# U and V's halves loaded with a cast by GpSimd's queue, two steps moved to GpSimd, and a new written-out order, in an attention and mixer kernel

## The chip, the cores and the metric

The kernel runs on one core of a Trainium2 chip. The metric is the device time of one execution in microseconds (us), as a median of several runs. A profile shows one execution: TensorE (PE, with its weight loads PEld), VectorE (DVE), ScalarE (ACT), GpSimd (POOL) and the DMA queues of SyncE (SP) and of GpSimd.

## The reference

Causal local attention with a few global keys, then a mixer over tokens of low rank, then an MLP. Cut to what matters:

```python
B, H, S, D = 4, 8, 768, 64          # n_global = 8, n_local = 96, rank = 32
keep = is_global | is_local          # a query sees 96 keys back and the first 8
scores = where(keep, scale * q @ k.T - slope[h] * dist, -1e9)
a = softmax(scores)
x = (a @ v)                          # [B, S, 512], heads side by side
h = x.transpose(0, 2, 1) @ U @ V     # U [768, 32], V [32, 768]
u = x + h.transpose(0, 2, 1)
out = u + relu(u @ w_ch1) @ w_ch2    # w_ch1 [512, 2048], w_ch2 [2048, 512]
```

## The kernel before

All work is cut into some 1100 named steps, each with an engine. A list, `ORDER`, names them all in one order; each engine runs its own steps in the order in which they stand in that list. A planner in the kernel walks the list with a cost for each step. It gives each step a start, PSUM banks and buffers, and puts filler matmuls on zeros (L1327, function `idle`) where it expects PE to wait in the early part. The dictionary `CFG` holds a letter for each choice of engine (A ACT, D DVE, P GpSimd, S a DMA by SP, Q a DMA by GpSimd).

The work goes over 4 batches, and in a batch over 4 pairs of heads, p = 0 to 15. The steps of a pair p, with the lines at which they show in the profile:

- `lk`, `lq`, `lv`: loads of k, q and v, cast from float32 to float16 by DMAs of GpSimd's queue (L450 for pairs 1 to 3, L454 as two halves of 96 KB for later pairs, L458 for v). Pair 0 comes in float32 by SP (L468) and is cast by `Ck`, `Cq`. Buffers are few (3 for q, 3 for k), so a load waits for an earlier pair's transpose. At most 8 DMAs of a queue are under way.
- `TK`, `TQ`: transposes on PE (L594, L575 for pairs 1 to 3). `EK`, `EQ`: their eviction from PSUM (L359 on ACT, L361 on DVE, a helper's lines). `KO`, `VC`, `VG`: copies of k and v for the blocks off the diagonal.
- `SB` (L697, pairs 0 to 3, the bias by a matmul), `S` (L716, scores in three groups .0 to .2), `EX` (L781, exp on ACT), `MK` (mask by DVE, from pair 4 on).
- `PV` (L848, L849), `RC` (reciprocal), `NM` (L887, normalisation into `x_sb`), `XC` (cast of x to float16, `x16`). The last pair of batch 0 does this in thirds (`PV3.0`, `RC3.0`, `NH3.0`, ...).
- `UP`: on PE, x is transposed (L822) and multiplied with U. There are two forms. For the pairs in `CFG["NU"]` x is the stationary operand and U moves, 32 columns at a time (L827); then come `XE`, an eviction into `xus`, and `XU`, one transpose (L928). For the others U, repeated four times, is stationary and x moves, 128 columns at a time (L832).
- `TE`: eviction of x'U into `tmp`. `HM` (L946): times V, added onto the transposed x. With letter R in `CFG["HR"]` its two halves use 64 rows each and run side by side on PE, with F they use all rows one after the other. `E0`, `E1`: eviction of the sum into `uT`.

Changing between matmuls on all rows and matmuls on half the rows costs PE a short pause.

Then the batch's MLP. `M1a` to `M1d` are the first product (L1000 for halves, L1024 for the four blocks done at full width), `RL`, `RM` its ReLU on ACT. Half of it in batches 1 and 2 and three quarters in batch 3 goes by a Strassen-like scheme (`ZP`, L1095, with sums `ZU` to `ZX`, `ZA` to `ZR`). The second product is in seven parts `P1` to `P7` (L1226) of three row blocks, with `RS` (L1218) ahead, `PA`, `PB` for sums, and `DA` to `DH` (L1238, L1265, L1278) adding onto `x_sb`. `O` stores a row block (SP). The weights come in quarters, `w1_0` to `w1_3` (L503) and `w2_0` to `w2_3` (L506), through GpSimd's queue between the pairs' loads. `CFG["OS"]` lists stores that are issued in two pieces.

U and V: `mixl` loads both in float32 by SP (L509, L510) into a part of `x_sb`. `u16` (ACT) makes the float16 copy of U, four times. `vz` clears `vs`, and `vs0`, `vs1`, `vs2` fill it: V's halves, and their difference (L521). `back` is a small memset that ties `mixl` to a place in the order.

GpSimd's queue at first, before: `ones2 wz iota lk1 ones0 lq1 lk3 lq2 ones3 lv0 lk2 lq3 ones1 lv1 lk5 lv3 lv2 lq5 lk4 lq4 w1_0 lk7 w1_3 lv4 lq6 w1_2 lq7 w1_1 lk6 lv5`.

PE at first, before: `... TQ3 SB2.1 S2.1 SB2.2 S2.2 PV1 SB3.0 S3.0 SB2.0 S2.0 SB3.1 S3.1 SB3.2 S3.2 TK5 TQ5 PV2 UP0 TK4 UP1 HM0 PV3.0 PV3.1 PV3.2 TQ4 UP2 HM1 HM2 UP3.0 UP3.1 UP3.2 M1a0.3 M1c0.3 HM3 S4.1 M1d0.3 TK7 M1b0.3 ...`

Of the kernel before, what the change touches and what calls it, by code (L numbers as in the profile page):

```python
# [21 lines left out]
lk0 ones2 wz iota lq0 lk1 ones0 vz relf lq1 rel3 lk3 lq2 bias1 ones3 lv0 bias0 SB0.2 SB0.1 Ck0.1 Cq0.0 bias2 bias4  # L22
Ck0.0 TK0 EK0.1 lk2 Cq0.1 TQ0 EQ0.0 SB0.0 lq3 EK0.0 KO0.1 KO0.0 EQ0.1 mask1 S0.0 EX0.0 TK1 S0.1 EX0.1 EK1 S0.2 KO1
TQ1 EQ1 ones1 lv1 back SB1.1 TK3 EK3 KO3 VC0 mask5 VG0 EX0.2 lk5 lv3 lv2 lq5 lk4 SB1.2 S1.1 EX1.1 S1.2 TQ2 EQ2 lq4
SB1.0 w1_0 S1.0 EX1.0 TK2 EK2 KO2 lk7 VC1 w1_3 PV0 RC0 EX1.2 lv4 VG1 TQ3 EQ3 SB2.1 S2.1 EX2.1 lq6 SB2.2 S2.2 EX2.2
PV1 NM0 SB3.0 S3.0 EX3.0 RC1 NM1 SB2.0 S2.0 w1_2 EX2.0 mixl u16 XC0 VC2 VC3 VG3 SB3.1 S3.1 EX3.1 SB3.2 S3.2 EX3.2
VG2 vs0 vs1 TK5 EK5 XC1 TQ5 PV2 RC2 NM2 UP0 TE0 TK4 EK4 UP1 TE1 XC2 EQ5 HM0 E00 PV3.0 PV3.1 PV3.2 RC3.2 RC3.0 NH3.2
TQ4 EQ4 NH3.0 UP2 TE2 HM1 E01 HM2 E02 RC3.1 NH3.1 KO4 NM3 UP3.0 UP3.1 UP3.2 TE3 M1a0.3 M1c0.3 mask0 HM3 E03 KO5 S4.1
E13 EX4.1 lq7 M1d0.3 TK7 M1b0.3 RL0.3 M1b0.14 M1b0.15 M1a0.2 M1c0.2 M1a0.15 EX4.2 M1a0.13 vs2 TD0 M1a0.14 MK4.2 VC4
VG4 w1_1 RM0.15 RM0.14 RL0.15 mask2 S4.0 EX4.0 MK4.1 EK7 M1d0.2 M1b0.2 RL0.2 MK4.0 RL0.14 M1b0.13 mask3 KO7 ZS5  # L30
M1a0.10 M1b0.12 RM0.12 RM0.13 RL0.10 TQ6 PV4 M1a0.11 M1b0.11 RL0.13 EQ6 RC4 NM4 XC4 TQ7 EQ7 ZS7 RL0.11 RM0.11 lk6
lv5 S5.0 S5.1 EX5.0 MK5.0 EX5.2 M1a0.8 M1b0.10 RM0.10 PA0.3 PB0.3 M1a0.9 RL0.9 w2_2 EX5.1 MK5.1 M1b0.5 RM0.5 M1a0.0
M1c0.0 w2_0 M1d0.0 M1b0.0 MK5.2 VC5 VG5 TK6 EK6 RL0.8 M1a0.4 M1b0.4 RL0.0 M1b0.7 RM0.7 w2_1 w2_3 ZS6 M1b0.6 UP4 PV5
RM0.6 XE4 KO6 RL0.4 M1b0.8 RM0.4 XU4 TE4 lv7 M1a0.5 RM0.8 M1a0.6 RC5 NM5 TWa0 TWb0 RL0.6 M1a0.7 M1a0.1 M1c0.1 M1d0.1
M1b0.1 RL0.7 RL0.5 PA0.1 RL0.1 PA0.0 M1b0.9 RM0.9 M1a0.12 S7.0 RL0.12 PB0.1 PA0.2 PB0.2 EX7.0 RS0.0 HM4 E04 P10.0
XC5 P20.0 S6.1 EX6.1 EX6.2 RS0.1 P10.1 P20.1 UP5 XE5 PB0.0 TWa1 DA0.0 TWb1 lq8 TQ8 EQ8 lk8 TK8 EK8 lq10 P30.0 DF0.0
XU5 DA0.1 P30.1 DF0.1 mask4 MK6.1 MK6.2 P50.0 lv6 lq9 VC7 TE5 HM5 mask6 KO8 S6.0 EX6.0 E05 P60.0 DB0.0 lk9 mask7
lk10 lv8 P60.1 DB0.1 lv11 S7.1 RS0.2 EX7.1 MK6.0 MK7.0 EX7.2 MK7.2 P10.2 P70.0 TK9 EK9 TQ9 EQ9 MK7.1 VC6 DA0.2 VG6
TQ10 EQ10 P50.1 TK10 EK10 P70.1 DC0.0 lq11 VG7 PV7 DD0.1 KO9 PV6 RC7 NM7 P20.2 XC7 lk11 RC6 NM6 P60.2 DB0.2 P30.2
UP7 XC6 VC8 VG8 P40.1 UP6 P70.2 XE6 XU6 TE6 ZS4 XE7 XU7 lk12 TE7 DD0.0 P40.0 DC0.1 O0.1 HM6 E06 HM7 E17 DF0.2 DG0.1  # L40
ZP11.5 DD0.2 P40.2 ZU1.5 DG0.0 E07 ZT1 S8.0 EX8.0 S8.1 O0.0 EX8.2 EX8.1 KO10 P50.2 M1a1.3 TK11 DC0.2 EK11 O0.3
ZP11.4 ZU1.4 DG0.2 ZP61.5 ZW1.5 ZP21.5 ZA1.5 O0.2 O0.4 M1b1.3 RL1.3 KO11 TQ11 lq13 ZP61.4 ZW1.4 EQ11 ZP21.4 ZA1.4
ZP51.5 MK8.0 MK8.2 S9.1 EX9.1 ZP71.4 ZX1.4 ZP71.5 ZX1.5 M1a1.7 EX9.2 ZP51.4 ZB1.4 ZB1.5 M1a1.6 ZP41.4 ZR1.4 ZP41.5
ZR1.5 MK8.1 RL1.6 ZP31.4 ZP31.5 ZD1.4 ZP11.6 ZU1.6 ZP21.6 M1b1.7 RL1.7 PV8 ZD1.5 lv10 RM1.7 ZP11.7 ZU1.7 M1b1.6
MK9.2 ZP61.6 ZW1.6 M1a1.2 M1b1.2 RM1.6 ZP61.7 RL1.2 MK9.1 ZP71.6 ZW1.7 M1a1.4 RL1.4 ZA1.6 O0.5 RC8 ZQ1.5 NM8 XC8 UP8
XE8 ZQ1.4 PA1.1 lv9 VC10 VC9 S9.0 EX9.0 lv12 ZP21.7 ZP71.7 ZX1.7 ZV1.4 ZV1.5 PA1.2 PB1.2 XU8 TE8 M1b1.4 RM1.4 M1b1.5
RM1.5 ZP51.6 HM8 E08 ZA1.7 ZX1.6 TK12 TD1 EK12 ZP41.7 ZR1.7 M1a1.5 RL1.5 VG9 ZB1.6 ZP51.7 ZB1.7 M1a1.0 ZV1.6 M1b1.0
RL1.0 ZV1.7 ZP31.6 M1a1.1 M1b1.1 MK9.0 lq12 TQ12 ZP31.7 VC11 ZP41.6 VG11 ZD1.6 ZQ1.6 EQ12 ZD1.7 ZQ1.7 RL1.1 ZR1.6
PA1.3 RS1.1 S10.1 EX10.2 EX10.1 PA1.0 PB1.0 S10.0 EX10.0 PB1.3 KO12 P21.1 P11.1 PV9 P51.1 RC9 NM9 PB1.1 DA1.1 S11.0
EX11.0 RS1.0 P21.0 P51.0 P11.0 DA1.0 XC9 S11.1 EX11.2 EX11.1 MK11.0 P31.0 DF1.0 MK11.2 P61.1 MK10.0 UP9 XE9 lq14  # L50
TQ14 EQ14 MK11.1 P31.1 DF1.1 P61.0 DB1.0 XU9 TE9 PV11 RC11 lk14 TK14 EK14 lk15 HM9 DB1.1 P71.0 E09 P71.1 lv14 VC14
S12.0 EX12.0 RS1.2 NM11 KO14 DD1.1 DC1.0 P11.2 lk13 DD1.0 S12.1 EX12.1 EX12.2 P41.0 P21.2 MK10.1 VG10 MK10.2 PV10
TK13 EK13 DA1.2 XC11 VC12 DG1.0 P31.2 RC10 TQ13 P61.2 NM10 XC10 DF1.2 VG14 UP11 DB1.2 DC1.1 O1.1 EQ13 UP10 lq15
MK12.2 P71.2 XE11 XU11 XE10 DD1.2 XU10 KO13 TE10 P41.1 DG1.1 HM10 TE11 TD2 E010 HM11 E011 E111 ZT2 S14.0 EX14.0
P51.2 ZP12.6 ZU2.6 P41.2 DC1.2 O1.4 DG1.2 O1.3 S14.1 EX14.1 MK14.1 EX14.2 MK14.2 M1a2.1 M1b2.1 RL2.1 ZP62.6 ZW2.6
M1b2.5 RM2.5 TQ15 TK15 M1b2.4 EK15 M1a2.5 KO15 RM2.4 ZP12.7 RL2.5 ZP52.6 EQ15 ZU2.7 O1.5 ZP72.6 ZX2.6 M1a2.4 M1a2.3
M1b2.3 MK12.0 VG12 MK12.1 PV12 ZB2.6 ZP32.6 ZV2.6 MK14.0 RL2.4 RL2.3 RC12 ZD2.6 ZP62.7 ZP22.7 ZW2.7 ZP12.4 ZA2.7
ZP52.7 ZP42.6 ZU2.4 ZP72.7 ZR2.6 ZP62.4 ZP22.6 ZX2.7 M1a2.0 M1b2.0 O1.2 O1.0 NM12 ZB2.7 ZP32.7 ZA2.6 XC12 ZQ2.6 lv15
VC15 VG15 ZW2.4 PV14 ZD2.7 ZP12.5 RC14 ZP72.4 RL2.0 NM14 XC14 UP12 XE12 ZU2.5 ZP22.5 ZA2.5 PA2.0 ZP62.5 ZW2.5 ZX2.4
M1a2.7 ZP22.4 ZA2.4 XU12 TE12 ZP72.5 ZP52.4 ZB2.4 ZV2.4 ZP42.7 RL2.7 ZV2.7 HM12 ZR2.7 ZQ2.7 ZP42.4 M1a2.2 ZX2.5 E012  # L60
M1b2.2 RL2.2 PA2.3 ZP42.5 ZR2.5 ZP52.5 ZB2.5 ZP32.4 ZD2.4 ZQ2.4 ZV2.5 UP14 XE14 M1b2.7 ZR2.4 RM2.7 ZP32.5 XU14 TE14
ZD2.5 ZQ2.5 M1b2.6 RM2.6 PA2.2 PB2.2 M1a2.6 RL2.6 HM14 E014 RS2.1 P12.1 S13.1 EX13.1 PA2.1 RS2.0 P12.0 DA2.0 P22.0
P22.1 EX13.2 P62.0 P52.1 S15.1 EX15.2 PB2.3 PB2.0 PB2.1 DB2.0 DC2.1 P32.0 DA2.1 P72.0 MK13.1 DF2.0 P32.1 DF2.1
EX15.1 P62.1 MK15.1 lv13 S13.0 S15.0 EX15.0 MK13.2 MK15.2 RS2.2 P12.2 MK15.0 P52.2 EX13.0 MK13.0 P32.2 PV15 DD2.0
P22.2 VC13 VG13 PV13 DA2.2 P62.2 DB2.1 P72.1 RC15 NM15 XC15 UP15 RC13 NM13 XC13 UP13 DB2.2 P72.2 DD2.1 XE15 XU15
XE13 XU13 DF2.2 ZS3.3 TE15 P52.0 DD2.2 ZS3.2 HM15 TE13 HM13 TD3 E115 P42.1 DG2.1 P42.2 E013 ZP13.5 ZP13.2 ZU3.2 E015
P42.0 ZT3 ZP13.4 M1a3.0 ZU3.4 ZU3.5 O2.1 ZP63.2 ZW3.2 DG2.0 DC2.2 DC2.0 O2.3 O2.2 DG2.2 O2.5 M1b3.0 ZP63.5 ZP23.2
ZA3.2 RL3.0 ZP63.4 ZP73.2 ZW3.4 ZP13.3 ZU3.3 ZP23.4 ZA3.4 ZP23.5 ZW3.5 ZA3.5 ZP73.4 ZP13.7 ZX3.2 ZX3.4 ZU3.7 ZP63.3
ZW3.3 ZP53.4 ZB3.4 M1a3.1 M1b3.1 RL3.1 ZP63.7 ZP73.5 ZX3.5 ZP33.4 ZD3.4 ZQ3.4 ZP73.3 ZX3.3 ZP53.5 ZB3.5 ZV3.5 ZP53.3
# [35 lines left out]
class Planner:  # L105
# [57 lines left out]
    def run(self, names):  # L163
        if sorted(names) != sorted(self.names):
            raise RuntimeError("order and tasks differ")
        clock = {PE: 0.0, ACT: 2.0, DVE: 0.7, POOL: 0.75, SP: 0.7}
        lanes = {POOL: [0.0] * self.LANES, SP: [0.0] * self.LANES}
        mode = 0
        dma_free = {POOL: 6.1, SP: 0.0}
        shared_port = {POOL: [], DVE: []}  # L170
        for t in (self.names[n] for n in names):
            r = 0.0
            for d in t.deps:
                r = max(r, d.end + (0.0 if t.eng == d.eng and d.size == 0.0 else d.lat))
            r = max([r] + [g.read for g in t.bw] + [g.written for g in t.br])
# [6 lines left out]
            if t.size:  # L182
                r = max(r, lanes[t.eng][t.parts - 1])
# [1195 lines left out]
```

## Time and profile before

| | |
|---|---|
| time, median of 3 runs | 225.0 us (224.84 to 225.39) |
| the profiled execution | 225.68 us, span of the trace 223.9 us |
| PE, DVE, ACT, POOL busy | 217.5, 182.3, 143.5, 68.9 us |
| PE clock granted | 1.00 |
| DMA | 23.97 MB, 107 GB/s on average; 160 to 200 GB/s in the first 67 us |

The span runs from the first to the last instruction of the trace; the execution's time has 1.8 us more around it. A busy PE includes filler and the modelled ends of matmuls. For each group the page gives its count, the busy time, the mean of one, and what ended the idle time before it. The landing time of a DMA is when the last of its 16 parts has arrived.

### The profile page before, as it was taken

To read this page: it belongs to the slowest core of one execution; us is meant where nothing else is said; L and a number is where in the kernel's file an instruction comes from. 1 tells how busy PE (TensorE), PEld (TensorE's weight loads), DVE (VectorE), ACT (ScalarE), POOL (GpSimd) and SP (SyncE) were. 2 spreads that over 40 slices of the span, in tenths; PEclk is the share of its full clock that TensorE was granted. 3 is DMA by queue.
4 is the path that set the end of the run, shared out by engine and by line. 5 is a ranking of instruction groups with operands and counts; after the bars stand their busy time and mean duration, and the time that the engine had idled before them with its cause. 6 is when DMAs were issued, how large, how long until landed. Compare 5 with 4: busy or idle time off the path is not lost.

```text
span 223.9 us, 6008 instructions
## 1 busy us (share of the span) xinstructions
PE 217.5 (97%) x2446; PEld 160.8 (72%) x2446; DVE 182.3 (81%) x407; ACT 143.5 (64%) x251; POOL 68.9 (31%) x90
## 2 busy tenths in 40 slices
PE   8997999999999999999999999999999999999993
PEld 3754876675888976666788886666688976658883
DVE  5876957889998887997987888788888995888892
ACT  6889697887877378787855567668732347882000
POOL 8876976634964400191221400012000000000000
PEclk9999999999999999999999999999999999999999
DMA  6999999999999987399090941609100104000035
GB/s 172 174 176 146 181 182 185 193 206 161 169 149 73 157 151 223 97 115 71 0 107 12 108 123 52 200 12 70 39 3 3 47 3 187 0 4 0 0 116 215
DMA packets 88763, 23.97 MB, mean 107 GB/s; under 512 B 76416, under 2 KB 86528, under 8 KB 88736
## 3 DMA queue, kind: packets, MB, share of 16 engines
q0 software_dynamic: 69888, 13.64, 73.8%
q1 hardware_dynamic: 18848, 9.95, 15.7%
q8 instruction: 19, 0.31, 0.6%
q14 instruction: 8, 0.07, 0.1%
HBM read 27.46 MB, written 6.29 MB: 151 GB/s over the span
## 4 chain that ended last, share of the span: by engine, by line
PE 90%; DMA 4%; POOL 2%; issue 1%; ACT 1%; DVE 0%; DVEq 0%; POOLq 0%
PE ps L1226 34%; PE ps L1095 14%; PE ps L1000 13%; PE ps L1024 8%; PE ps L716 4%; DMA stgq<-in_q_dram 4%; PE ps L594 4%; PE ps L822 3%; PE ps L849 2%; PE ps L848 2%; PE ps L946 2%; PE ps L1327 1%; PE ps L1218 1%; PE ps L697 1%; POOL stgk L454 1%
## 5 line engine op out<-in xcount | busy, mean ns | idle before, releaser
L781 ACT ACTIVATE ep<-ps 128x1024 f16<-128x1024 f32 (+1 forms) x48 | 43.9, 952 | 14.8 <-PE ps L716 14.5
L1226 PEld LDWEIGHTS <-htr 128*128 128x128 f16 x392 | 36.2, 98 | 6.7 <-issue 2.3
L1238 DVE TENSOR_TENSOR x_sb<-x_sb,ps 128x256 f32<-128x256 f32 (+1 forms) x60 | 26.9, 464 | 7.5 <-PE ps L1226 7.1
L1000 PE MATMUL ps<-uT,w 128*128 128x384 f16 x176 | 32.4, 326 | 0.0
L1226 PEld LDWEIGHTS <-sA 128*128 128x128 f16 x288 | 27.3, 98 | 3.5
L458 POOL DMA_DIRECT2D vt<-in_v_dram x16 | 16.6, 1046 | 30.7 <-PE ps L849 27.3
L1000 PEld LDWEIGHTS <-w 128*128 128x128 f16 x176 | 16.7, 98 | 10.5
L1226 PE MATMUL ps<-w,sA 128*128 128x256 f16 x192 | 24.2, 273 | 0.0
L1226 PE MATMUL ps<-tB,htr 128*128 128x256 f16 (+1 forms) x200 | 23.8, 268 | 0.0
L1226 PE MATMUL ps<-w,htr 128*128 128x256 f16 x192 | 23.5, 273 | 0.0
L1006 ACT ACTIVATE htr<-ps 128x384 f16<-128x384 f32 x44 | 20.8, 492 | 4.1 <-PE ps L1000 3.5
L454 POOL DMA_DIRECT2D stgk<-in_k_dram x24 | 19.8, 845 | 9.9 <-PE ps L594 5.0
L454 POOL DMA_DIRECT2D stgq<-in_q_dram x24 | 20.0, 844 | 5.6 <-DMA w<-in_moe_w_ch_dram 3.4
L1024 PE MATMUL ps<-uT,w 128*128 128x384 f16 x112 | 21.3, 326 | 0.0
L1113 DVE TENSOR_TENSOR htr<-ps,zu 128x384 f16<-128x384 f32 x30 | 16.1, 554 | 6.1 <-PE ps L1095 4.6
L794 DVE TENSOR_TENSOR ep<-ep,mask 128x1024 f16<-128x1024 f16 x24 | 15.9, 684 | 2.9 <-ACT ep L781 2.9
L359 ACT ACTIVATE zu<-ps 128x384 f32<-128x384 f32 x30 | 14.4, 492 | 4.2 <-PE ps L1095 4.0
L887 DVE TENSOR_TENSOR x_sb<-ps,rcp 128x768 f32<-128x768 f32 x16 | 15.2, 953 | 0.4
L1024 PEld LDWEIGHTS <-w 128*128 128x128 f16 x112 | 10.6, 98 | 6.8
L1095 PEld LDWEIGHTS <-w 128*128 128x128 f16 x108 | 10.1, 98 | 6.2 <-issue 0.3
L1042 ACT ACTIVATE htr<-ps 128x768 f16<-128x768 f32 x14 | 11.3, 811 | 4.7 <-PE ps L1024 4.5
L716 PE MATMUL ps<-qT,kT 64*128 64x128 f16 x192 | 14.0, 217 | 0.0
(127 smaller groups left out, 442.3 us busy)
## 6 DMA issues: line engine op xcount, KB each, us to landing
out_dram<-x_sb SPq DMA_DIRECT2D x17, 256.0 KB, 2.4
w<-in_moe_w_ch_dram POOLq DMA_DIRECT2D x8, 512.0 KB, 10.6
vt<-in_v_dram POOLq DMA_DIRECT2D x16, 192.0 KB, 6.6
stgk<-in_k_dram POOLq DMA_DIRECT2D x24, 96.0 KB, 5.8
stgq<-in_q_dram POOLq DMA_DIRECT2D x24, 96.0 KB, 6.1
out_dram<-x_sb SPq DMA_DIRECT2D x13, 128.0 KB, 1.9
vo<-vt SPq DMA_DIRECT2D x8, 165.0 KB, 2.5
kO<-kT SPq DMA_DIRECT2D x6, 120.0 KB, 2.7
```

What stands on the lines that cost most here:

```text
L454: nc.gpsimd.dma_start(o[:, i], src[b, h0 + i].rearrange("(n p) d -> p n d", p=P))
L458: nc.gpsimd.dma_start(vt[gv.slot][:, :, :, 0:D], v[b, h0:h0 + 2].rearrange("h (n p) d -> p h n d", p=P),)
L716: nc.tensor.matmul(t[:, hi, j * P:(j + 1) * P], lhs, qt[r, i * P:(i + 1) * P], start=not biased, stop=True, skip_group_check=biased,)
L781: nc.scalar.activation(ep[gep.slot][:, :, lo:512], ps[:, gsc.slot:gsc.slot + 2, lo:512], AF.Exp, scale=qk_scale)
L794: nc.vector.tensor_tensor(ev, ev, mv, ALU.mult)
L1000: nc.tensor.matmul(ps[:, g.slot, 0:HS], w1[:, dc, jt * P:(jt + 1) * P], ub[:, dc, i * HS:(i + 1) * HS], start=(dc == 0), stop=(dc == NDC - 1),
L1006: nc.scalar.activation(htr[:, jt, i * HS:(i + 1) * HS], ps[:, g.slot, 0:HS], AF.Relu)
L1024: nc.tensor.matmul(ps[:, g.slot + half, 0:HS], w1[:, dc, jt * P:(jt + 1) * P], ub[:, dc, half * HS:(half + 1) * HS], start=(dc == flat[0]) ...
L1095: nc.tensor.matmul(bank(g), a()[:, i], bq[:, i], start=first and i == 0, stop=last and i == 1, skip_group_check=True,)
L1113: return lambda: nc.vector.tensor_tensor(o, x(), y(), ALU.add)
L1226: nc.tensor.matmul(o if part is None else o[:, part], a[:, j, c0 + cols.start:c0 + cols.stop], bq[:, j] if part is None else bq[:, j, part ...
L1238: nc.vector.tensor_tensor(o, o, x, ALU.add)
```

## The change

U is loaded by one DMA of GpSimd's queue straight into `u16` with a cast, without the fourfold copy (`CFG["U16"]` A to Q). V's halves come likewise into `vs` (`vs0`, `vs1`: Q); `vs2`, the difference, is built on GpSimd (P) from V, which `mixl` still loads in float32, later. All 16 pairs are in `NU`, so pairs 0 to 3 take the form of `UP` with `XE` and `XU` (eight new steps). `HM` of pairs 2, 9 and 12 goes from F to R. x of pair 2 is cast by GpSimd (`XC`: P). Several evictions change between ACT and DVE, two more stores are split, and `ORDER` is written anew. The planner is told of one more rule on DMA issues and a start of 5.6 instead of 6.1 for GpSimd's queue. `RC` names the `NM` two pairs earlier, on the same engine, as an input.

```diff
-    "NU": (4, 5, 6, 7, 8, 9, 10, 11, 12, 13, 14, 15),
+    "NU": (0, 1, 2, 3, 4, 5, 6, 7, 8, 9, 10, 11, 12, 13, 14, 15),
...
-    "OS": ((0, 0), (0, 1), (0, 2), (0, 3), (0, 4)),
-    "ZR": "DDAADDDA", "TE": "ADAAAAAAAAAAAADA", "XE": "DDDDDAADADAADAAA", "EK": "ADDDDDADADADDAAD", "EQ": "DDAAAADDAAADDAAD", "KO": "ADDDDDADSSSSASDS",
-    "HR": "FRFRRRRRFFRRFRRR", "U16": "A", "VS": "DAD", "C0": "ADDADADA", "EKS": "ADDADADA", "EQS": "DDDADADA", "KOS": "ADDADADA",
-    "VO": "DDDDDDDSSSSSDSSS", "XC": "DDDDDAAADADQADQA", "E": "AAAAAAAAAAAAAAAA",
+    "OS": ((0, 0), (0, 1), (0, 2), (0, 3), (0, 4), (0, 5), (1, 0)),
+    "ZR": "DDDDADDD", "TE": "ADDDAAAAAAAAAADD", "XE": "DAAAAAAAAAADAAAA", "EK": "ADDAAADDAAADAAAD", "EQ": "DDDADDDDAAADDAAA", "KO": "ADDDADSDSSASSSAS",
+    "HR": "FRRRRRRRFRRRRRRR", "U16": "Q", "VS": "QQP", "C0": "DDADDADA", "EKS": "DADADADA", "EQS": "AADADADA", "KOS": "DDDADADA",
+    "VO": "DDDDDDASSSSSSSAA", "XC": "DDPDDADADADQAAQD", "E": "AAAAAAAAAADAAAAA",
...
     def load_mixer():
-        nc.sync.dma_start(uf, moe_U.rearrange("(c p) r -> p c r", p=P))
+        if not uq:
+            nc.sync.dma_start(uf, moe_U.rearrange("(c p) r -> p c r", p=P))
         nc.sync.dma_start(vf, moe_V)
...
+            if e is None:
+                nc.gpsimd.dma_start(o, moe_V[:, g * HS:(g + 1) * HS])
...
+        c_u16 = add(
+            POOL, 0.84, lambda: nc.gpsimd.dma_start(u16[:, :, 0], moe_U.rearrange("(c p) r -> p c r", p=P)), size=0.8, name="u16",
+        )
```

The new order, engine by engine, where the text speaks of it:

- GpSimd: `ones0 wz iota lk1 lq1 lk2 lq2 lv0 lk3 ones2 ones1 lv1 u16 vs0 lq3 lv2 lq5 ones3 lv3 lk5 lk4 vs1 lq4 w1_3 lk7 XC2 lq7 w1_0 lq6 w1_2 lv4 lk6 w1_1 lv5 w2_0 vs2 w2_2 w2_1 w2_3 lk8 ...`
- PE: `SB0.2 TK0 SB0.1 SB0.0 TQ0 TK1 S0.2 S0.0 TQ1 S0.1 TK2 SB1.1 SB1.0 S1.0 S1.1 TQ2 SB1.2 S1.2 PV0 TK3 SB2.0 S2.0 SB2.1 S2.1 SB2.2 S2.2 TQ3 PV1 SB3.1 SB3.0 S3.1 S3.0 PV2 SB3.2 S3.2 UP0 UP1 TK5 PV3.0 PV3.1 XU0 TK4 XU1 TQ5 HM0 PV3.2 HM1 UP2 UP3.0 UP3.1 UP3.2 XU2 XU3 TQ4 HM2 HM3 S4.1 TK7 S4.0 M1a0.15 M1b0.15 M1b0.12 M1b0.14 TQ7 M1b0.13 M1a0.2 ...`, and at the end `... P33.1 P43.0 P43.2b P43.2a P43.1` (before: `... P73.2 P43.0 P43.1 P43.2a P43.2b`)
- ACT after the first exp: `EX0.2 EX0.0 EX0.1 EX1.0 EX1.1 EX1.2 EK3 EX2.0 EX2.1 EQ3 EX2.2 EX3.1 EX3.0 EX3.2 XE1 EK5 TE0 EK4 E00 E01 XE2 XE3 KO4 E02 E13 EX4.2 ...` (before: `EX0.0 EX0.1 mask5 EX0.2 EX1.1 EQ2 EX1.0 EX1.2 EQ3 EX2.1 EX2.2 EX3.0 EX2.0 u16 EX3.1 EX3.2 vs1 TE0 EQ5 E00 EQ4 TE2 E01 E02 TE3 mask0 E13 EX4.1 ...`)
- DVE there: `... NM2 VC3 VG3 XE0 back RC3.0 RC3.1 NH3.1 TE1 EQ5 NH3.0 RC3.2 NH3.2 NM3 TE2 TE3 EQ4 E03 ...`
- SP: the last stores are `O3.5a O3.5b O3.5c O3.4` (before: `O3.5a O3.3 O3.4 O3.5b O3.5c`).

## The prediction

> **What bounds the kernel now.** I read the page first (busy shares, slices, DMA issues), then the chain of waits in order of time, then PE's timeline where the chain left PE, then ACT's timeline and the landing times of the DMAs in the trace.
>
> ```profile
> PE 217.5 (97%) x2446; PEld 160.8 (72%) x2446; DVE 182.3 (81%) x407; ACT 143.5 (64%) x251; POOL 68.9 (31%) x90
> PE   8997999999999999999999999999999999999993
> DMA  6999999999999987399090941609100104000035
> ```
>
> PE is full in every slice but the first, the fourth and the last, and the DMA engines are full until about 80 us. So time is to be had in two ways: less work on PE, or fewer holes in its first 30 us.
>
> ```profile
> 11.76 0.59 POOL vt L458
> 12.86 0.94 POOL stgq L454
> 13.80 8.81 DMA stgq<-in_q_dram
> 22.74 0.50 PE ps L594 x6
> ```
>
> The chain has one long piece that is not PE: the two halves of lq5 are issued from 12.86 and land at 22.60; TQ5 waits for them. PE's timeline shows that hole and the other gaps:
>
> ```profile
> 14.69 0.53 PE L575 MATMUL ps<-ident,stgq 128*64 128x128 f16 x12 [0.48 <-DMA stgq<-in_q_dram]
> 22.74 0.50 PE L594 MATMUL ps<-ident,stgq 128*128 128x128 f16 x6 [1.55 <-DMA stgq<-in_q_dram]
> ...
> 26.74 0.34 PE L1327 MATMUL ps<-zero 128*128 128x128 f16 x3
> ...
> 27.95 0.52 PE L1327 MATMUL ps<-zero 128*128 128x128 f16 x6
> ...
> 29.95 0.34 PE L1327 MATMUL ps<-zero 128*128 128x128 f16 x3
> ```
>
> L1327 is filler, idle time that looks busy: 0.9 us with the gaps around it. From the first SB0.2 (3.09) to the first MLP matmul (29.30) PE takes 26.2 us. Adding up its real work there by the rows (SB 0.43 or 0.32, TK or TQ 0.34, a score group 0.17 or 0.23, PV 0.67, UP 0.67, HM 0.17 or 0.33, each change of row mode 0.097) gives 20.2. So 6.0 us are not work. After 30 us no gap between matmuls exceeds 0.1 us: there only PE's work counts.
>
> Two feeders stand behind the holes. ACT runs from its first exp (8.04) to the last exp of pair 3 (22.48) with under 1 us of waits, and again up to E13 (30.62 to 31.11). And the load queue serves in order: lk2 lands at 12.31, lv2 at 21.31. Its five loads between would take 0.96 + 4 x 1.27 = 6.0 by their undisturbed neighbours (9.06 to 10.02, 10.02 to 11.29), not 9.0. The other 3.0 are these two, which run beside them:
>
> ```profile
> x_sb<-in_moe_U_dram SPq DMA_DIRECT2D x1, 96.0 KB, 7.0
> x_sb<-in_moe_V_dram SPq DMA_DIRECT2D x1, 96.0 KB, 7.6
> ```
>
> **The change part by part.**
>
> *PE's work.* With all pairs in NU, UP of pairs 0 to 3 takes 0.49 (UP4, 49.11 to 49.60) instead of 0.667 (UP0, 23.75 to 24.41), plus one XU of 0.055: 4 x 0.12 = -0.5. HM of pairs 2, 9 and 12 turns from F to R: 0.325 (25.42 to 25.74) becomes 0.17 (30.22 to 30.39): 3 x 0.155 = -0.5. Counted in the written order, changes of row mode fall from 77 to 74: -0.3. Together -1.3, all on the path, since PE is.
>
> *U and V.* U becomes one DMA of 768 pieces. Its nearest row is a half load of L454, also 768 pieces; two halves are served in 1.28 (lk7, 27.08 to 28.36), so one in 0.64; low end 0, high end 1.3. vs0 and vs1 have 32 rows each; between 0 and 0.63, I take 0.2. V whole (mixl) still goes through SP, but now behind TK5. At the point where the second batch of loads is through, the queue is 3.0 - 0.64 - 0.2 - 0.2 = 2 us less loaded, 1 at the least: lk5, last of that same set in the new order, lands near 20.8 instead of the 22.6 of lq5.
> By the Trainium skill ("DMA: Bandwidth & Descriptors", Specifications) transfers below 512 B are read, modified and written, so U's rows of 64 B would cost more than their bytes say. The trace agrees in kind: 96 KB in pieces of 128 B took 0.64, 512 KB of weights 2.56. If the smaller pieces doubled the row, an estimate by that page, lk5 would land 0.6 later, TK5 would feel 0.4 of it, and the sum would be -1.9 instead of -2.3.
>
> *GpSimd's queue.* It gains three issues (0.7 to 0.84 by L450 and L454), XC2 and vs2. No row has a GpSimd cast; the same cast takes 0.62 on DVE and 0.85 on ACT, and iota (256 columns in 0.33) scales to 0.99. I take 0.9, range 0.6 to 2. vs0's DMA waits for the memset vz, moved behind KO0.1 on DVE (about 7.5); behind it wait lq3, lv2, lq5. GpSimd gets there after 8.3, so nothing. XC2 waits for NM2; behind it wait lq7, w1_0, lq6, w1_2. By my walk below NM2 ends near 20.8, GpSimd has issued lk7 by 21.7, and XC2 ends at 22.6, before UP2 (23.8). vs2 has 25 us to RS0: nothing.
>
> *ACT up to E13.* It loses u16 (0.83), vs1 (0.52), EQ2, EQ4 and EQ5 (0.81 each), TE2 and TE3 (0.28 each), two masks to the time ahead of the first exp (0.5 each); it gains XE1 to XE3 (0.28 each), EK3, EK4, EK5 (0.81 each) and KO4 (0.9). From first exp to E13: 20.7 busy before (of 23.1), 19.5 after. Were its 2.4 us of waits to stay, E13 would end at 30.0; with none at 27.6.
>
> *The walk.* I followed the new order with the rows' durations, each step starting at the later of its engine and its inputs. TK1 waits for lk1 (7.07), so the first exp starts at 8.2; exps follow almost without waits, EX3.2 ends near 21.3 (22.48 before). PV2, UP0 and UP1 stand ahead of TK5 now and fill the time in which PE waited for lq5. TK5 runs at 21.1, PV3.0 at 21.6 (25.74 before, as it stood behind the hole), PV3.2 at 23.4 (TK4 before it waits for lk4, 22.0), NH3.2 ends at 24.8, UP3.2 at 25.1. Here the change adds a step: XE3 on ACT, XU3 on PE, 0.8 with the hops. TE3 26.4, HM3 26.9, E13 28.2. Meanwhile PE does S4.1, TK7 and S4.0, which stood behind the first MLP matmuls. M1a0.15 starts at 28.4 with 20.6 us of work behind it: 28.4 - 3.1 - 20.6 = 4.7 not work, against 6.0. That is -1.3; between -2.1 (E13 at 27.6, PE then the limit) and +0.3 (E13 at 30.0).
>
> *Weights.* w1_0 moves from first to second behind w1_3, and behind lq7. By the queue's pace (w1 2.56, pair 1.27) it lands at 31.1; M1a0.2 comes at 28.4 + 3.6 = 32.0. w1_2 lands at 35.0, M1b0.11 is at 36.2. Covered by 1 us; past that each us costs one.
>
> *The body.* DVE's and ACT's shares shift by a few us over 180 (ACT +4, DVE -3 by the rows). Loaded in order against PE, neither exceeds PE over a stage, as before: 0, with 0 to +2 for a stray wait.
>
> *Tail.* The last PE step becomes P43.1, and the last store the whole O3.4 instead of a quarter row. O3.4 took 2.03 from issue to landing, O3.5c 1.68; DVE's part after the last matmul was 0.5 (two pieces) and is 0.42 to 0.46 (one). +0.3; 0 to +0.7 by the median row of 256 KB (2.4).
>
> Sum: -1.3 - 1.3 + 0.3 = -2.3. Profiled execution: 225.68 (span 223.9 and 1.8 around it) to 223.4; the median, 0.7 below the profiled one, 225.0 to 222.7.
>
> **The rivals.**
> - *The early gain fails to come.* ACT keeps its waits, E13 is at 30.0. Against it: those waits were for score groups behind loads. -1.3 + 0.3 + 0.3 = -0.7: 224.3. Chance 0.13.
> - *GpSimd's cast holds DVE.* XC2 and DVE use SBUF at once; if DVE stands still for those 0.9 us while RC3, NH3 and EQ5 wait, E13 slips by 0.9: -1.4, 223.6. For it: DVE is then the fuller engine (6.1 of 6.3 us from 23.0 to 29.3). Against: DMA issues on GpSimd took 821 to 945 ns whatever DVE did. Chance 0.10. The Trainium skill ("SBUF — State Buffer", Who interferes with whom) has the pair of ports shared by the two as an exclusive lock, the later one blocked wholly, which speaks against this cast; no run shows a case of it yet.
> - *Slower: GpSimd stands at XC2 and the weights come late.* Everything behind XC2 waits for NM2. If NM2 ends at 25.2, as it does now, w1_0 is issued at 25.2 + 0.9 + 1.7 = 27.8 and, taking 6.9 as now (20.16 to 27.08), lands at 34.7: M1a0.2 stalls 2.7 and the gain is gone (225.4). With NM2 at 27, 4.5 are lost: 227.2. It decides from NM2 at 25.3 on. For it: PE's order is strict, and one late load ahead of PV2 moves NM2. Against: PV2 now stands ahead of TK5. Chance 0.12.
> - *In-order waits in the body*, new places where PE meets a late relu or a full bank, 2 to 4 us over 180: 224.5 to 227. For: every order from 30 us on is new. Against: the present one shows none. Chance 0.12.
> - That U's new path isn't taken can't be: the CFG letters select it.
>
> **How the numbers follow.** My forecast has 0.53. What a measurement of this kernel tells from no change is 0.3%, 0.7 us: 224.3 to 225.7. Faster: 0.53 + 0.10 + half of the early rival (0.06) + 0.02 of the body, 0.71. Same: the other half, 0.03 of the XC2 rival and 0.01 of the body, 0.11. Slower: 0.09 of each of these two, 0.18. The range goes from 221.6 (ACT with few waits, a shorter tail) to 225.8.
>
> **What would show it.** Right: L832 gone, L827 x96, L928 x16; no hole over 0.5 us at TK5 or TQ5; first L1000 matmul near 28.4 (31.93 before); XC2 ended by 23; w1_0 landed by 32; the last DMA 0.3 longer. Wrong: PE waiting on w before 37 us, filler near 25 to 30 as long as now, DVE steps beside XC2 stretched, or new gaps after 40 us.

## The result, and the profile after

The changed kernel takes 227.11 us (median of 17 runs, 225.38 to 229.03). The kernel before, run beside it on the same chip, takes 225.49 (17 runs, 224.84 to 226.69). The ratio is 1.0058, 95% interval 1.0036 to 1.008: slower by 0.6%, where 1% faster was forecast. The profiled execution took 226.29 with a span of 224.5 (before: 225.68 and 223.9). Times of the changed kernel also scatter twice as far.

The page of the changed kernel, in the order of the lines shown of before (busy time, PE and DMA by slice, and the shares of the chain):

```profile
PE 215.1 (96%) x2419; PEld 158.3 (71%) x2419; DVE 179.6 (80%) x400; ACT 146.4 (65%) x257; POOL 72.7 (32%) x95
...
PE   7799999999998999799999999999999999999993
...
DMA  6999999999999999849259522508100016000025
...
PE 68%; DMA 24%; POOL 2%; DVE 1%; issue 1%; SPq 1%; ACT 1%; POOLq 0%
PE ps L1244 27%; PE ps L1113 12%; DMA vo<-vt 12%; PE ps L1018 9%; DMA vt<-in_v_dram 7%; PE ps L1042 6%; DMA stgk<-in_k_dram 6%; PE ps L732 3%; PE ps L610 2%; PE ps L865 2%; PE ps L838 2%; PE ps L864 2%; PE ps L1236 1%; SPq L366 1%; PE ps L964 1%
```

PE is busy for 2.4 us less than before, filler included. The dent of the fourth slice has gone. The first two slices are emptier (7 and 7 instead of 8 and 9), and two new dents stand at slices 13 and 17, about 70 and 92 us. In slices 15 to 17, from 78 to 95 us, the DMA engines are at 9, 9 and 8 tenths, where before they fell to 8, 7 and 3. A transfer that hardly mattered before, `vo<-vt`, holds 12% of the chain. (Lines have moved: L1000 is now L1018, L1226 is L1244, L1095 is L1113, L848 and L849 are L864 and L865, L594 is L610, L575 is L591, L359 and L361 are L362 and L364, L1327 is L1345.)

The early part came out nearly as forecast. PE's timeline there (start, duration, form, what ended the idle time):

```profile
21.95 0.50 PE L610 MATMUL ps<-ident,stgk 128*128 128x128 f16 x6
22.28 0.34 PE L1345 MATMUL ps<-zero 128*128 128x128 f16 x3
...
26.00 0.34 PE L1345 MATMUL ps<-zero 128*128 128x128 f16 x3
...
28.87 2.77 PE L1018 MATMUL ps<-uT,w 128*128 128x384 f16 x16
```

The first row is TK5, the last the first MLP matmuls of the new order. What PE waits for, over the whole span (total, times, longest), has a new first line; before had no wait of PE on `vo` in this list:

```profile
PE ps L864 <- DMA vo<-vt: 2.0, 3, 0.8
```

These are PV7 at 70.55 and PV8 at 91.24. The chain, in order of time, shows how each came about:

```profile
58.20 6.01 DMA vo<-vt
64.28 0.70 SPq L366
65.03 6.60 DMA vo<-vt
71.68 0.19 PE ps L864
...
78.31 0.59 SPq L366
78.99 7.63 DMA vo<-vt
86.64 0.65 SPq L366
87.33 5.74 DMA vo<-vt
93.12 0.19 PE ps L864
```

Each pair of transfers is VC followed by VG, issued by SP, each waiting for the one ahead: VC7, VG7, then VC8, VG8. In the kernel before, VG7 landed at 71.0 and PV7 came at 72.48; VG8 landed at 81.1 and PV8 came at 93.03. So the one chain had 1.5 us of slack and the other 12.

Where the 0.6 us went can be added up from the matmul records. "Work" is all matmuls but filler, with gaps up to 0.14 us. "Not work, early" is filler and longer gaps up to the first L1018 matmul (L1000 before), "holes after" the same behind it. Each column is one profiled execution. The last column is the best-understood experiment, told below.

| us | before | after | later loads |
|---|---|---|---|
| start to first matmul | 0.94 | 0.94 | 0.94 |
| work | 211.21 | 209.74 | 209.86 |
| not work, early | 8.19 | 7.14 | 7.40 |
| holes after | 0 | 2.77 | 0.96 |
| last matmul's start to the end | 3.58 | 3.92 | 3.91 |
| span | 223.9 | 224.5 | 223.1 |

PE's work is 1.47 less, the early part 1.05 less, the tail 0.34 more, and the body 2.77 more: +0.6. This accounts for the two profiled executions; the medians lie 1.6 apart, and for the other 1.0 us there is no trace.

The DMA engines between 76 and 94 us, before and after (40 slices of the window; share of 16 engines by queue, q1 is SP's and q0 GpSimd's; a share adds up the time that packets took and can exceed 100%):

```profile
DMA  9999999761088717978887782797979561002020
...
q1 hardware_dynamic: 5513, 2.35, 46.7%
q0 software_dynamic: 3610, 0.46, 39.7%
```

```profile
DMA  9999999999999999999999999999999999999428
...
q0 software_dynamic: 9876, 1.24, 107.6%
q1 hardware_dynamic: 5396, 2.38, 55.6%
```

SP moves the same 2.4 MB in both. GpSimd's queue moves 1.24 MB instead of 0.46: lq13, lk14, lq12, lk12 and lk15 are issued from 75.8 to 85.7, since the new order has no waiting load ahead of them. Before, the last loads to leave were lv10 and lv9 (73.6, 74.6), and then lv12, next in the queue, waited for PV8's buffer until 94.2; everything behind it came at 95 to 101. In the same window SP's stores took three times as long, first before, then after (KB each, median us from issue to landing):

```profile
out_dram<-x_sb SPq DMA_DIRECT2D x10, 128.0 KB, 1.9
```

```profile
out_dram<-x_sb SPq DMA_DIRECT2D x12, 128.0 KB, 5.9
```

The Trainium skill ("DMA: Bandwidth & Descriptors", Queues, rings and completion order) says that each DMA engine takes turns between the queues that have work for it, a packet at a time. The two rows agree with it, as stores on another queue than the loads take longer beside them, but they do not show the turns themselves.

### The profile page after: what moved, and what is told of

Same layout as the page of the kernel before. It is cut to its first block, busy times and chain, and to the rows that moved or that the text cites. A ratio compares the mean times of both kernels' runs of the same rounds, so it can differ in the third digit from the quotient of the medians.

```text
span 224.5 us, 5965 instructions
## 1 busy us (share of the span) xinstructions
PE 215.1 (96%) x2419; PEld 158.3 (71%) x2419; DVE 179.6 (80%) x400; ACT 146.4 (65%) x257; POOL 72.7 (32%) x95
## 4 chain that ended last, share of the span: by engine, by line
PE 68%; DMA 24%; POOL 2%; DVE 1%; issue 1%; SPq 1%; ACT 1%; POOLq 0%
PE ps L1244 27%; PE ps L1113 12%; DMA vo<-vt 12%; PE ps L1018 9%; DMA vt<-in_v_dram 7%; PE ps L1042 6%; DMA stgk<-in_k_dram 6%; PE ps L732 3%; PE ps L610 2%; PE ps L865 2%; PE ps L838 2%; PE ps L864 2%; PE ps L1236 1%; SPq L366 1%; PE ps L964 1%
## 5 line engine op out<-in xcount | busy, mean ns | idle before, releaser
L797 ACT ACTIVATE ep<-ps 128x1024 f16<-128x1024 f32 (+1 forms) x48 | 43.4, 953 | 12.2 <-PE ps L732 11.9
L1244 PEld LDWEIGHTS <-htr 128*128 128x128 f16 x392 | 36.5, 98 | 6.0 <-issue 1.5
L1018 PE MATMUL ps<-uT,w 128*128 128x384 f16 x176 | 32.9, 326 | 0.0
L1244 PEld LDWEIGHTS <-sA 128*128 128x128 f16 x288 | 27.0, 98 | 3.9 <-issue 0.5
L457 POOL DMA_DIRECT2D stgk<-in_k_dram x24 | 20.3, 854 | 14.5 <-PE ps L732 11.2
L1244 PE MATMUL ps<-w,sA 128*128 128x256 f16 x192 | 24.4, 273 | 0.0
L1244 PE MATMUL ps<-tB,htr 128*128 128x256 f16 (+1 forms) x200 | 23.9, 268 | 0.0
L1018 PEld LDWEIGHTS <-w 128*128 128x128 f16 x176 | 16.6, 98 | 10.3
L1244 PE MATMUL ps<-w,htr 128*128 128x256 f16 x192 | 23.3, 273 | 0.0
L1042 PE MATMUL ps<-uT,w 128*128 128x384 f16 x112 | 20.8, 326 | 0.0
L362 ACT ACTIVATE zu<-ps 128x384 f32<-128x384 f32 x30 | 14.5, 491 | 6.9 <-PE ps L1113 5.8
L903 DVE TENSOR_TENSOR x_sb<-ps,rcp 128x768 f32<-128x768 f32 x16 | 15.3, 955 | 1.3 <-DMA out_dram<-x_sb 0.8
L1113 PEld LDWEIGHTS <-w 128*128 128x128 f16 x108 | 10.2, 98 | 6.3 <-issue 0.3
L865 PEld LDWEIGHTS <-ep 128*128 128x128 f16 x192 | 12.5, 97 | 2.7 <-issue 1.6
```

The source lines that it names most:

```text
L457: nc.gpsimd.dma_start(o[:, i], src[b, h0 + i].rearrange("(n p) d -> p n d", p=P))
L797: nc.scalar.activation(ep[gep.slot][:, :, lo:512], ps[:, gsc.slot:gsc.slot + 2, lo:512], AF.Exp, scale=qk_scale)
L865: nc.tensor.matmul(o, e[:, hi, (j + 1) * P:(j + 2) * P], vv[:, hi, i, 0:D1], start=(i == 0), stop=True)
L1018: nc.tensor.matmul(ps[:, g.slot, 0:HS], w1[:, dc, jt * P:(jt + 1) * P], ub[:, dc, i * HS:(i + 1) * HS], start=(dc == 0), stop=(dc == NDC - 1),
L1042: nc.tensor.matmul(ps[:, g.slot + half, 0:HS], w1[:, dc, jt * P:(jt + 1) * P], ub[:, dc, half * HS:(half + 1) * HS], start=(dc == flat[0]) ...
L1113: nc.tensor.matmul(bank(g), a()[:, i], bq[:, i], start=first and i == 0, stop=last and i == 1, skip_group_check=True,)
```

## The experiments

Two readings were to be told apart. One: VC8 and VG8 stand too late in SP's in-order queue (behind O0.0 and VC9, which wait for other things), and their place is the cause. The other: the burst of loads fills the DMA engines, and whatever SP has under way then is late. In the quoted expectations of the first four runs theory A is the place in SP's queue and theory B the full DMA engines; the later runs name them the other way round. All ratios are to the kernel before, run beside each set. Each figure for holes is of one profiled execution.

| run | median us | ratio, 95% interval | PE's holes after the first L1018 matmul, us |
|---|---|---|---|
| e1_vc8 | 226.76 | 1.0066 [1.0045, 1.0087] | 1.65 |
| e2_vc8_vo7 | 226.58 | 1.0066 [1.0039, 1.0094] | 1.54 |
| e3_half | 225.12 | 1.0003 [0.9981, 1.0026] | 1.34 |
| e4_all | 226.33 | 1.004 [1.0016, 1.0063] | 2.26 |
| e6_late | 224.79 | 0.9962 [0.994, 0.9985] | 0.96 |
| e7_late_all | 225.0 | 0.9991 [0.9967, 1.0016] | 0.52 |
| e8_before_uv | 229.13 | 1.0166 [1.0141, 1.0191] | 0 |
| e9_before_uv_vo7 | 230.26 | 1.0214 [1.0192, 1.0236] | 1.17 |
| e10_late_xc2d | 225.48 | 1.0003 [0.9979, 1.0028] | 0.26 |
| e11_late_tail | 224.83 | 0.9977 [0.9962, 0.9991] | 0.29 |
| e12_late_lv7 | 224.62 | 0.9955 [0.993, 0.998] | 0.59 |

**VC8 and VG8 earlier in SP's queue.** The orders of the other engines stay.

```diff
-... S7.1 VG7 lk11 ... XE7 KO9 DB0.2 ... HM7 VC8 lq13 ... O0.5 VG8 M1a1.3 ...
+... S7.1 VG7 VC8 lk11 ... XE7 KO9 VG8 DB0.2 ... HM7 lq13 ... O0.5 M1a1.3 ...
```

> The changed kernel with one edit in SP's queue: VC8 right behind VG7 and VG8 right behind KO9, so both ahead of O0.0 and VC9; every other engine's queue is the same. Theory A (the loss is SP's queue: VC8 and VG8 stand behind O0.0 and VC9, and PE waits 1.76 us for them at PV8): that hole vanishes, the one at PV7 (1.01 us) stays, 227.1 - 1.8 = 225.3. Theory B (the DMA engines are so full that any early gain is handed back): the hole reappears within the next pairs, 226.5 to 227.1. Theory C (GpSimd's cast and difference or the weights behind it cost the time): no difference, 227.1.

PV8's hole went, but the time did not come down: 226.76. Another one took its place, in rows of DVE and then of PE:

```profile
95.16 0.96 DVE L903 TENSOR_TENSOR x_sb<-ps,rcp 128x768 f32<-128x768 f32 x1 [1.96 <-DMA vo<-vt]
```

```profile
96.17 0.81 PE L1018 MATMUL ps<-uT,w 128*128 128x384 f16 x4 [0.96 <-DVE x_sb L903]
```

L903 is NM8. It writes into the `x_sb` of batch 0, whose stores must have landed first: the first piece of O0.3 landed at 94.9 (before, the last store of the batch landed at 89.9; the `vo` that the row names is what the profile inferred, and the chain names stores at that place, issued from 82.35 on). This is the case that the expectation gave for theory B. So the place in the queue alone is not the cause: with it mended, the stores are late instead.

**The same, and VC7 and VG7 copied by DVE.** VC7 also moves in the order, to stand next to VG7.

```diff
-    "VO": "DDDDDDASSSSSSSAA",
+    "VO": "DDDDDDADSSSSSSAA",
```

> As the run with VC8 and VG8 moved, and besides the copies VC7 and VG7 by DVE (0.33 and 0.3 us, next to each other at the place of VG7) instead of two DMA hops by SP. Theory A: both holes vanish, 227.1 - 2.8 = 224.3 if DVE's 0.7 us are hidden, 225.0 if not. Theory B: 226 or more, PE waiting somewhere else. Theory C: 227.1.

PV7 no longer waits for a copy (0.28 us is left there), and NM8 waits for the stores again: 0.87 on PE at 93.8. A new wait of 0.4 on w1 at 32.4 comes with it. The time hardly moved, 226.58.

**Half of the late loads left out.** Of pairs 12 to 15 only the first head's half of q and k is loaded; nothing else changes.

```diff
-                    for i in range(2):
+                    for i in range(1 if p in (12, 13, 14, 15) else 2):
```

> The changed kernel with the second head's half of each q and k load of pairs 12 to 15 left out (part of the computation is changed): the burst of loads at 76 to 86 us is halved, SP's queue is as in the changed kernel. If VC8's place in the queue alone made the hole at PV8, it stays (VC8 issued at 79.0): 227.0. If it takes the burst as well, VC8 lands in 4.4 us as in the kernel before instead of 7.6, VG8 by 88, and the hole vanishes: 225.3. Theory B expects less too, 224 to 225.5, since the DMA engines have less to do.

225.12, 2.0 us below the changed kernel by the medians and some 1.2 by the ratios, with PV8's hole gone, although VC8 and VG8 stand where the change put them (VC8 still took 7.6 us, VG8 2.6 and 2.0 instead of 5.6 and 5.7). This points at the burst, but it also moves fewer bytes.

**All of it, with the end in another order.**

```diff
-... P43.0 DD3.1 O3.2a DD3.2 P43.2b DF3.1 O3.1 DG3.0 O3.3 O3.5a P43.2a P43.1 DG3.2a O3.5b DG3.2b O3.5c DG3.1 O3.4
+... P43.0 DD3.1 P43.1 O3.2a DD3.2 P43.2b DF3.1 O3.1 DG3.0 DG3.1 O3.3 O3.4 O3.5a P43.2a DG3.2a O3.5b DG3.2b O3.5c
```

> As the run with VC8, VG8 and the pair 7 copies changed, and besides the last PE steps in the order P43.0, P43.1, P43.2b, P43.2a, so that a quarter row is stored last as before. Theory A: 0.3 less than without that, 224.0. Theory B or C: 0.3 less than whatever the former gives.

226.33. NM8 waited longest here, DVE's row shows for what:

```profile
94.48 0.96 DVE L903 TENSOR_TENSOR x_sb<-ps,rcp 128x768 f32<-128x768 f32 x1 [2.57 <-DMA out_dram<-x_sb]
```

PE lost 1.75 by it. The end, 3.97 us from the start of the last matmul, was hardly shorter than the 4.10 of e2_vc8_vo7.

**The same bytes, later.** Only GpSimd's order: lv12, which waits for PV8's buffer, goes ahead of lq13 and lk14, as a gate.

```diff
-... HM7 VC8 lq13 DC0.1 O0.4 O0.1 lk14 DG0.0 ... RL1.6 PV8 RC8 ... ZV1.7 lv12 VC12 ...
+... HM7 VC8 DC0.1 O0.4 O0.1 DG0.0 ... RL1.6 PV8 lv12 lq13 lk14 RC8 ... ZV1.7 VC12 ...
```

> Only GpSimd's order is changed: lv12 right behind PV8, and lq13 and lk14 behind it, so that these loads leave GpSimd at about 93 us instead of 75.8 to 78.3 (lq12, lk12, lk15 then follow lv12 too, since the queue is in order: only what stands ahead of lv12 goes early). Theory A (the burst of q and k loads of pairs 12 to 15 at 76 to 92 us shares the DMA engines with VC8, VG8 and the stores of batch 0, and stretches them): VC8 lands by 83.5 instead of 86.6, PV8 waits under 0.5 us instead of 1.8, NM8 waits for no store; 227.1 - 1.8 = 225.3, range 224.8 to 225.9. Theory B (the place of VC8 and VG8 in SP's queue): PV8 still waits over 1 us, 226.7 to 227.3.

224.79, 2.3 us below the changed kernel (2.2 by the ratios) and 0.4% below the kernel before. The same window of 76 to 94 us, then PE's only wait on `vo`:

```profile
DMA  9999999999999999999999941311698887726510
...
q0 software_dynamic: 5515, 0.69, 60.1%
q1 hardware_dynamic: 5520, 2.45, 54.4%
```

```profile
PE ps L864 <- DMA vo<-vt: 0.6, 2, 0.3
```

lq12 and lk12 still leave early; the rest leaves at 93.7. The engines have room from 86 us on. PV8 does not wait, and NM8 starts 0.04 us after its reciprocal. The stores of the window took 4.0 us in the median, between the 1.9 of before and the 5.9 of the changed kernel. One detail of the expectation was wrong: VC8 lands at 86.0, hardly before the 86.6 of the changed kernel; it is VG8 that shrinks, from 5.6 and 5.7 us to 2.1 and 1.9, and so lands at 88.1 and 88.6 instead of 92.2 and 93.1. The times also lie close together again (224.44 to 225.45 in 11 runs).

With e2_vc8_vo7 and the next run this closes a square of two by two: loads early or late, and copies of pairs 7 and 8 as in the changed kernel or both moved. Loads early: holes at 91 to 96 us with either (1.76 us and 0.87; e1_vc8, with only pair 8 moved, has 1.13). Loads late: none with either. The burst is the cause of these holes; the place in the queue decides which wait they show in.

**Later loads, VC8 and VG8 earlier, VC7 and VG7 by DVE:** the edits of e2_vc8_vo7 and e6_late together.

> The same as the run before it, and VC7, VG7 copied by DVE, VC8 and VG8 earlier in SP's queue. Theory A: neither PV7 nor PV8 nor NM8 waits; both holes of the changed kernel (1.0 and 1.8 us) are gone: 227.1 - 2.8 = 224.3, range 223.8 to 225.2. Theory B, or a third wait that nothing has shown yet: 226 to 227.

The body's holes are down to 0.52, as expected, but the median is 225.0, not 224.3 (224.48 to 227.53): what PV7 no longer loses is not seen in the median. In its profile the early gaps (without filler) fell to 3.63 us from the 4.88 of e6_late, but the early work rose from 20.9 to 22.1. Until about 10 us PE ran at about half pace there: the four SB matmuls of 512 columns that start at 5.53 took 1.70 us, and the same four took 0.92 in e6_late (at 5.01).

**The change's U, V and PE parts in the order of before.** Letters and order of before, but U and V by GpSimd's queue, all pairs in `NU`, `HR` of the change. The planner is that of the change too.

```diff
-... lv1 back ... mixl u16 XC0 ... VG2 vs0 vs1 TK5 ... UP0 TE0 TK4 EK4 UP1 TE1 XC2 ... E00 PV3.0 ... UP2 TE2 HM1 E01 HM2 ... UP3.2 TE3 M1a0.3 M1c0.3 ...
+... lv1 u16 vs0 vs1 back ... mixl XC0 ... VG2 TK5 ... UP0 XE0 TK4 EK4 XU0 TE0 UP1 XE1 XC2 ... E00 XU1 TE1 PV3.0 ... UP2 XE2 HM1 E01 XU2 TE2 HM2 ... UP3.2 XE3 M1a0.3 M1c0.3 XU3 TE3 ...
```

> The order and the letters of the kernel before, with only these parts of the change: U and two halves of V by GpSimd's queue (issued behind lv1), all pairs in NU with XE and XU of pairs 0 to 3 put behind their UP, and HM of pairs 2, 9 and 12 in form R. If the U and V edit and PE's saved work are good by themselves and only the new order costs: 225.5 - 1.3 (PE's work) - 0.5 to 1.0 (TQ5's hole) = 223.5, but PV7 had 1.5 us of slack to VG7's landing (72.48 against 71.0), so that 224.0 holds if VG7 does not come earlier; range 223.0 to 224.6. If the three issues that GpSimd's queue gains delay the loads that follow by as much as they save: 224.7 to 225.7 with a hole at TQ5 or TK5 as before.

229.13: both expectations missed. PE's timeline has most of the reason, the filler:

```profile
20.86 1.10 PE L1345 MATMUL ps<-zero 128*128 128x128 f16 x16
...
22.14 1.93 PE L1345 MATMUL ps<-zero 128*128 128x128 f16 x30
...
25.39 1.22 PE L1345 MATMUL ps<-zero 128*128 128x128 f16 x18
```

TQ5 between them runs at 21.80, 0.94 earlier than before: the lighter load queue does work in the old order too. But then 30 fillers run to 23.9, although pair 2's copies of v had ended at 22.07. Filler is a count fixed beforehand from the planner's costs, so it stays where the wait has gone, and with the short gaps ahead of it it takes 10.1 us up to the first L1018 matmul (34.92), against 4.7 before up to the first L1000 (31.93). XU0 waited for XE0, which stands behind NM2 on DVE. Behind the first L1018 matmul there was no hole. So in this order and with this filler the parts do not gain. No run shows how much of the added filler comes from the planner's new rule on DMA issues and not from the parts, or what the parts would give with less filler.

**The same, with VC7 and VG7 by DVE.** VC7 again moves next to VG7.

> The run before it, and VC7 and VG7 copied by DVE instead of by a DMA of SP. If the copies of pair 7 limit the run before (PV7 waits there): 0.3 to 0.8 us less than that, 223.3. If PV7 does not wait there: the same within 0.3, or up to 0.3 more for DVE's 2 copies.

230.26: PV7 now waits 1.0 us for DVE's copy. Neither case was expected; DVE has no room there in this order.

**Later loads, x of pair 2 cast by DVE.**

```diff
-    "XC": "DDPDDADADADQAAQD",
+    "XC": "DDDDDADADADQAAQD",
```

> The kernel with the later loads (224.8), and x of pair 2 cast by DVE instead of GpSimd. If GpSimd's cast of 0.84 us held DVE still, or delayed the loads behind it in GpSimd's queue: 0.3 to 0.9 us faster, first MLP matmul 0.5 or more earlier, 224.2. If it does not: DVE, the fuller engine there, gains 0.6 us of work, the first MLP matmul comes 0 to 0.6 later: 224.8 to 225.4.

225.48, against 224.79 with the cast on GpSimd. The ratios, 1.0003 and 0.9962, differ by about as much as their intervals are wide, and these are runs of two sets: no harm by GpSimd's cast is seen, and a gain is not shown either. The profile cannot price the cast, as PE had half its clock for some 7 us there, told at the end.

**Later loads, the end in the order of before** (the edit of e4_all's last lines).

> The kernel with the later loads (224.8), and the end in the order of before: P43.0 P43.1 P43.2b P43.2a, and O3.4 ahead of O3.5a, so that the last store is a quarter row again. If the tail's new order costs what the trace shows (3.92 us from the start of the last matmul to the end, 3.58 before): 0.3 less, 224.5. If the difference lies in how long SP's last issues take and not in the order: 224.8, with the distance staying at 3.9.

224.83: no gain over 224.79. From the start of the last matmul to the end it took 3.8 us, 0.1 less, in one execution.

**Later loads, lv7 ahead of lv8 and VG7 ahead of VC10.**

```diff
-... PV5 RL0.7 lv8 ... UP4 lv7 M1a0.1 ... ZS7 VC10 EX6.0 ... S7.1 VG7 lk11 ...
+... PV5 RL0.7 lv7 ... UP4 lv8 M1a0.1 ... ZS7 EX6.0 ... S7.1 VG7 VC10 lk11 ...
```

> The kernel with the later loads (224.8), lv7 ahead of lv8 in GpSimd's queue and VG7 ahead of VC10 in SP's. lv7 landed at 58.1 and lv8 at 56.7, VC7 leaves when lv7 has landed and takes 6 us, VG7 leaves when VC7 has landed. If PV7's wait (0.96 us beyond its matmuls) comes down this chain: lv7 lands near 57, VC7 near 62.8, VG7 near 70, PV7 waits under 0.3: 224.1, range 223.8 to 224.5. If VC7 and VG7 take the longer the earlier they start, because the DMA engines are full until 73: VG7 lands at 71 or later again and the time stays at 224.6 to 225.0.

224.62 (223.52 to 225.64 in 12 runs), the lowest median, 0.5% below before, but not told apart from e6_late. In the profiled execution lv7 landed at 58.15 and VC7 at 64.55, as without the edit: all loads from w1_0 on were late there by up to 1.8 us (w1_0 landed at 33.96, at 32.19 in the changed kernel). VG7 landed at 71.6 and 71.9, which is the second case of the expectation, and so is the time. PV7 did not wait, but PE had lost 1.06 at TK7 and 0.6 at w1 by then and so came later to it. So it leaves open how much of PV7's 0.96 this edit wins.

## Why the prediction was wrong

By its own steps:

- *PE's work, -1.3:* right. The records give -1.47.
- *The early part, 6.0 to 4.7, -1.3:* nearly right, -1.05 by the records. The first MLP matmul of the new order came at 28.87 where the walk had 28.4. U was served in about 0.33 us behind the load ahead of it (14.10 to 14.42), not 0.64. The row had been chosen by its number of pieces; U's 48 KB are half of that row's 96 KB and took half its time, so the bytes were the measure here, and smaller pieces did not double it. lk5 still landed at 21.8 and not 20.8, and TK5 ran at 21.95 (21.1). The expectation of `mixl` behind TK5 was wrong: V was loaded at 1.73 us, ahead of everything, as nothing ties it to its place any more: `back` writes where U used to land. New holes near 4 and 7 us (0.95 and 1.1) took part of the gain.
- *GpSimd's queue:* w1_0 landed at 32.19 instead of 31.1, and PE did not wait for it. So the rival of late weights fell.
- *XC2:* 0.84 us against 0.9, but it ended at 24.5, not 22.6, as the issue of lk7 stood ahead of it until 23.65.
- *XC2 holds DVE (a rival):* no. GpSimd's row, then DVE's copy beside it and one without it:

```profile
23.65 0.84 POOL L368 CAST x<-x_sb 128x768 f16<-128x768 f32 x1
```

```profile
23.97 0.55 DVE L364 COPY qT<-ps 128x768 f16<-128x768 f16 x1
...
26.93 0.56 DVE L364 COPY qT<-ps 128x768 f16<-128x768 f16 x1
```

  DVE's steps beside the cast read PSUM. The Trainium skill ("SBUF — State Buffer", Who interferes with whom) has the lock only where DVE takes two inputs from SBUF or uses both port pairs, so its rule, read in full, fits these rows and did not speak against this cast.
- *Tail, +0.3:* the size was right (+0.34), the reason only in part. With the old end put back the distance went from 4.10 us (e2_vc8_vo7) to 3.97 (e4_all) and from 3.91 (e6_late) to 3.80 (e11_late_tail): about 0.1, in single executions. Where the other 0.2 comes from is not shown, so that the size came out is partly luck.
- *The body, 0, with 0 to +2 for a stray wait:* this is the step that failed. It measured +2.77, beyond its own upper end, and new gaps after 40 us were the prediction's own sign of being wrong. It was costed by the loads of ACT and DVE against PE alone. It followed GpSimd's and SP's new order only as far as the first weights, though the change rewrites them to the end, and it took "no gap after 30 us" of the old kernel as a property of the body, not of its slack. The trace of before had the warning for whoever asks of each copy and store how long before its use it lands: VG7 landed 1.5 us ahead of PV7, and the batch's stores leave from 78 to 88 us, where the DMA row falls from 9 to 8, 7 and 3 and so has the room for them.
- *Sum:* -1.47 - 1.05 + 0.34 + 2.77 = +0.6 in the profiled execution. The medians differ by 1.6, since the changed kernel's profiled execution lies 0.8 below its median and that of the kernel before 0.2 above its own; what the slower executions lose is on no trace. With the burst moved away both differences are -0.8 to -0.9.

The rival that came true is the one of in-order waits in the body, 224.5 to 227, and not through a late relu or a full bank but through DMAs. The forecast range ended at 225.8, below what this rival and that of the late weights allowed by the prediction's own numbers (227 and 227.2). Of the 2.77 us, 1.76 are shown to be the burst's. The other 1.0 is lost at PV7. PV7 starts 1.9 us earlier (70.55 against 72.48), while its chain comes later than before: lv7 landed at 58.1 instead of 54.4, VC7 at 64.2 instead of 60.3, VG7 at 71.6 instead of 71.0. DVE's copies removed most of the wait in two runs, but no run turned that into a sure gain, and which part of the new order made the chain late stays open.

## What to carry to other kernels

When a change moves loads in an in-order queue, list for the whole span what else is under way on the DMA engines when they now start, and how long before its use each copy and store lands; a load that "waits for a buffer" may be the gate that keeps the engines free. A mended wait that leaves the time as it was points to a shared cause: move the suspected traffic itself, with the same bytes. And an early gain can be lost again where a chain behind it has little slack and does not come earlier too.

## What the runs showed of the hardware

A late load early on was followed by a slow clock. In the profiled execution of e10_late_xc2d lk1 landed at 8.85 us instead of 7.2; PE waited 2.5 us for it. The stretches there (length; PE, PEld, DVE, ACT and POOL busy; clock, DMA share, GB/s):

```profile
5.00:10.00 5.00, 2.55 (x35) 1.84 (x34) 2.55 (x8) 2.18 (x5) 3.63 (x7) 0.85 1.27 165
10.00:20.00 10.00, 10.00 (x144) 5.76 (x142) 7.83 (x17) 7.44 (x9) 8.61 (x12) 0.73 2.22 163
```

These are means: cut at 8.5 and 15.3 us, the granted clock is 1.00, then 0.50 for 6.8 us, then 1.00 again. This execution took 227.66, against a median of 225.48. The fall comes inside the wait. In the other profiles gaps of up to 1.3 us at that place were followed by no such fall; that the longer gap is the cause is a guess from one execution. PE also starts slowly: the first four SB matmuls of 512 columns took 1.88 us in the kernel before (at 3.09) against 0.92 for four at 5.01 in e6_late, and in e7_late_all the slow pace lasted to about 10 us, where the clock column still read 1.00. And the parts of one DMA can land far apart: the 16 parts of w1_0 arrived within 0.94 us in the changed kernel's profile and within 2.3 us in that of e12_late_lv7. Some of the scatter of these times may lie in such loads and in such stretches, and not in the order.
